# Chunked WKV attention into a gated MLP on one NeuronCore: the bonus term moved from v to the diagonal of the scores

## The chip, the cores and the metric

The program runs on one core of a Trainium2 chip. The metric is device time in microseconds of one execution, from launch to end. Three executions of the kernel before took 542.83, 542.98 and 543.75 us, so the median is 542.98 us.

## The reference

```python
# r, k, v: (4, 8, 768, 48); w, u: (8, 48); w_in: (384, 2048); w_out: (2048, 384)
for t in range(S):
    cur = einsum('bhd,bhe->bhde', u[None] * k_t, v_t)
    y[:, :, t] = einsum('bhd,bhde->bhe', r_t, state + cur)
    state = w[None, :, :, None] * state + einsum('bhd,bhe->bhde', k_t, v_t)
x = y.transpose(0, 2, 1, 3).reshape(3072, 384)
h = x @ w_in
out = (h * cos(h)) @ w_out
```

A recurrence over 768 time steps with a 48 by 48 state per head is followed by an MLP whose gate is h times cos h. The term with u, the bonus, reaches only the output of its own time step: for each time step and head it is the number a = sum over d of r u k, times the row v.

## The kernel before, in words

**Attention.** Time is cut into chunks of 128 steps; 4 batches of 6 chunks make 24 chunks, numbered i, with batch i mod 4 and place c = i div 4 in the batch. The function `chunk` (line 579) lays out one chunk for all 8 heads, as 4 pairs of heads. It loads k, r and v (lines 595 and 611), brings k and r with decays multiplied in to a layout with the head dimension on the partitions (kT, rT: on PE by transposes at line 653 for the first 12 chunks, on DVE at line 661 for the later 12), and lets PE make the scores, transposed, with 16 matmuls (`mm_a`, line 744). The scores of the even heads and the odd heads lie in two PSUM banks. A predicated copy on DVE (`mask`, line 750) writes the scores that lie strictly above the diagonal into a tile A in SBUF, which GpSimd had set to zero at the start (line 333). The output of the chunk, x transposed, is gathered in one PSUM bank from three parts: the bonus part, the part from the state z of earlier chunks (line 771, 24 matmuls, only where c is over 0), and A times v (`mm_x2`, line 784, 32 matmuls). From there it is split into a high and a low float32r half (lines 814 and 819), xh and xl. The state is brought on by 16 matmuls with k and v (line 830) and one or two DVE operations (lines 838 to 841).

**The bonus before.** Four elementwise steps make it: m = r times k (`o_m`, line 688), m times u (`o_mu`, line 717), a as the sum over each head (`o_a`, line 723), and m = v times a (`o_vm`, line 732; DVE for the first 12 chunks, GpSimd for the later ones). Then `mm_x` brings the 128 by 384 tile m into the PSUM bank with 3 PE transposes (line 763), ahead of the part from the state.

**MLP.** The 24 chunks form 8 blocks of 3 (384 tokens). A step is one block n and one 128-wide slice f of the hidden dimension: 9 matmuls give h (line 231), then ACT, DVE, ACT, ACT, DVE, ACT and DVE round the angle, reduce it, take its size, its sine, multiply the gate and split it into gh and gl (lines 242 to 251 and 942 to 948), and 9 matmuls add to the 3 accumulators (line 237). Each float32 product is made of three float32r products. Blocks 0 to 3 go through the slices in four groups (0 to 2, 2 to 5, 5 to 10, 10 to 16), since the weights are still being converted then; blocks 4 to 7 go through all 16 at once. The weights arrive as raw words and are converted by `conv` in 32 pieces (loads at 424 and 429, ACT 513, DVE 521 and 533, POOL 544, ACT 549, DVE 554).

**What sets the order.** Nothing is issued in the order in which it is written. Each operation is given to a planner (`Plan`, line 72) with an engine, a due time, a cost in us, a latency, the operations that it waits for and the buffers that it holds. The planner runs a list schedule: each engine takes, among the operations that could start earliest (within 0.01), the one with the lowest due time, and the resulting order is what each engine's queue gets, in order. Operations marked `port` are not planned beside each other, whether on DVE or POOL. Buffers are rings (2 for r, 3 for k and v, 4 for A, 8 for the general tile f that holds m, among others), and PSUM banks are handed out in the same way. Chunk i below 12 has due time -1.5 (12 - i) - 1; MLP step s has due time s. Ahead of the first h (line 1008) the gaps that the plan has on PE are filled with dummy matmuls (line 1002).

**The start.** DVE clears wr (line 339), SP loads w into it (line 348), PE transposes it (line 353), DVE raises it to powers (lines 361 to 368) and spreads them into the two decay tables decT_k (DVE, line 381) and decT_r (POOL, line 382). PE transposes decT_k and ACT copies it to dec_k (lines 390 and 394). u is spread to all partitions by a load (line 403). POOL makes the identity, clears the padding of the k, r and v tiles (`start_pool`), and then clears zt, makes the mask `upper` and clears A (`start_pool2`).

**The end.** Each finished accumulator is copied to SBUF (line 976 or 978) and stored: from SP where the group of slices began at slice 0 (line 984), which holds for the last block, else by an accumulating store from POOL (line 986).

Of the kernel before, what the change touches and what calls it, by code (L numbers as in the profile page):

```python
# [35 lines left out]
ON_DVE = (0, 0, 0, 12)  # L36
# [127 lines left out]
def kernel(  # L164
# [89 lines left out]
    with ExitStack() as actx:  # L254
# [63 lines left out]
        def start_pool2():  # L318
            for t in R_zt:
                nc.gpsimd.memset(t.ap, 0.0)  # L320

            nc.gpsimd.memset(upper, 1)
            nc.gpsimd.affine_select(
                out=upper,
                in_=upper,
                pattern=[[1, C]],
                compare_op=ALU.is_gt,
                fill=0,
                base=0,
                channel_multiplier=-1,  # L330
            )
            for t in R_A:
                nc.gpsimd.memset(t.ap, 0.0)

        def start_dve():
# [3 lines left out]
        o_wr = op(DVE, -100, 0.1, lambda: nc.vector.memset(wr, 1.0), lat=0.1)  # L339
# [9 lines left out]
            [o_wr],  # L349
# [3 lines left out]
        o_wT = op(PE, -95, 0.1, lambda: nc.tensor.transpose(b_w()[:, 0:NP], wr.rearrange("p j d -> p (j d)"), ident[0:NP, 0:NP]), [o_w, o_pool], [b_w], lat=0.3)  # L353
# [27 lines left out]
        o_dtk = op(DVE, -89, 0.6, lambda: spread_decay(nc.vector, decT_k, qk, rq), [o_pow])  # L381
        o_dtr = op(POOL, -89, 1.4, lambda: spread_decay(nc.gpsimd, decT_r, qr, pq), [o_pow])
# [9 lines left out]
        def tab_copy():  # L392
# [8 lines left out]
            -6.2,  # L401
# [177 lines left out]
        def chunk(i, due, xbuf):  # L579
# [60 lines left out]
            ahead = [o_pool, last_A[0]] if late else [o_pool]  # L640
# [6 lines left out]
            l_v = op(SP, due - 4.0, 1.35, load(vb, v), ahead, [vb], lat=2.6, line=ln)  # L647
# [24 lines left out]
            else:  # L672
                t_r = op(PE, due - 2.4, 0.43, tr(rTp, rb), [l_r], [rb, rTp, rT], lat=0.3)
# [24 lines left out]
            if first:  # L698
                t_k = op(PE, due - 2.5, 0.43, tr(kTp, kb), [l_k], [kb, kTp, kT], lat=0.3)
                e_k = op(  # L700
                    DVE,
                    due - 2.3,
                    0.62,
                    lambda: nc.vector.tensor_tensor(kT()[0:KP], cube(kTp)[0:KP], decT_k[0:KP], op=ALU.mult),
                    [t_k, o_dtk],
                    [kTp, kT],
                )
                o_kd = op(e2, due + 1.0, c2, decay_k, [t_k, o_m, o_dk], [kb], port=True)
            else:
                o_kd = op(e2, due - 2.7, c2, decay_k, [o_m, o_dk], [kb], port=True)  # L710
            if not first and not late:
                t_k = op(PE, due - 2.5, 0.43, tr(kTp, kb), [o_kd], [kb, kTp, kT], lat=0.3)
                e_k = op(ACT, due - 2.3, 0.5, lambda: nc.scalar.copy(kT()[0:KP], cube(kTp)[0:KP]), [t_k], [kTp, kT])
# [13 lines left out]
            e3, c3, n3 = on(3)  # L727
            o_vm = op(
                e3,
                due - 1.5,  # L730
                c3,
                lambda: n3.tensor_tensor(
                    heads(mb), vb()[:, :, 0:D], ab()[:, :, None].to_broadcast([P, H, D]), op=ALU.mult
                ),
                [o_a, l_v],
                [vb, ab, mb],
                port=True,
            )
# [7 lines left out]
            last_A[0] = o_A = op(PE, due - 1.7, 1.1, mm_a, [e_k, e_r], [kT, rT, *Ap, *A], lat=0.3)  # L746
# [7 lines left out]
            e_A = [op(DVE, due - 1.4 + 0.01 * j, 0.65, mask(j), [o_A, o_pool2], [Ap[j], A[j]]) for j in range(2)]  # L754
# [4 lines left out]
            def mm_x():  # L759
                x = xv()  # L760
                m2 = mb()
                for kk in range(NK):
                    nc.tensor.matmul(  # L763
                        x[:, kk, :], m2[:, kk * P : (kk + 1) * P], ident, is_transpose=True, start=(kk == 0), stop=False,
                        skip_group_check=True,
                    )
                if c:
                    for g in range(NK * 4):
                        p, s = divmod(g, 3)
                        gs = slice(G * (g % 4), G * (g % 4) + G)  # L770
                        nc.tensor.matmul(  # L771
                            x[gs, g // 4, :], zb()[:, p, G * s : G * s + G], rT()[0:KP, p, :], start=False, stop=False,
                            skip_group_check=True,
                        )

            def mm_x2():
                x = xv()
                for g in range(NK * 4):
# [4 lines left out]
                    for n, (j, at) in enumerate(parts):  # L783
# [4 lines left out]
                            start=False,  # L788
# [6 lines left out]
            if c:  # L795
# [6 lines left out]
            zbs = [zb] if c else []  # L802
            xo1 = op(
                PE,
                due - 0.7,
                0.42 + (0.8 if c else 0),
                mm_x,
                [o_vm, e_r, *e_A, *o_zt],
                [mb, rT, xp, *zbs],
                lat=0.3,  # L810
            )
            xo2 = op(PE, due - 0.65, 1.03, mm_x2, [xo1, l_v, *e_A], [vb, *A, xp], lat=0.3)
# [11 lines left out]
            if c < CPB - 1:  # L824
# [18 lines left out]
                zo = op(PE, due + 1.2, 0.5, mm_z, [o_kd, l_v, xo1], [kb, vb, zp], lat=0.3)  # L843
# [54 lines left out]
        for s, (n, f, f0, f1) in enumerate(steps):  # L898
# [62 lines left out]
            for t in range(nt):  # L961
# [6 lines left out]
                if f == f1 - 1:  # L968
# [13 lines left out]
                    def st(ob=ob, dst=dst, f0=f0):  # L982
                        if f0 == 0:
# [5 lines left out]
                        SP if f0 == 0 else POOL,  # L989
# [165 lines left out]
```

## Time and profile before

| | |
|---|---|
| median of three runs | 542.98 us (542.83 to 543.75) |
| the profiled execution, its own time | 543.04 us |
| its span, first to last instruction | 541.3 us |
| mean granted TensorE clock | 0.994 |
| PE matmul, busy | 525.1 us, 97% of the span |
| DVE, busy | 434.3 us, 80% |
| ACT, busy | 348.6 us, 64% |
| POOL, busy | 196.3 us, 36% |

The span is what the trace shows; 1.7 us of the execution's own time lie around it. Matmuls overlap in the pipeline, so the sum of their durations is more than PE's busy time, and the step from one start to the next is what a matmul takes of PE's time. In a row of the timeline stand the start in us, the duration in us, engine, line, operation, what is written and read, shapes and count, and in brackets the idle time of the engine ahead of it with what ended it. A merged row (x3) runs from the first start to the last end. In a row of groups the two numbers after the bar are the busy time of the group in us and the mean of one in ns.

### The profile page before, as it was taken

Reading aid. Unit: us, or ns where it says so; the run is one execution under the profiler, and the core shown is the slowest. Engines: PE = TensorE matmul, PEld = TensorE weight load, DVE = VectorE, ACT = ScalarE, POOL = GpSimd, SP = SyncE. Lnnn points to the kernel's source line nnn. Section 1 sums busy time; section 2 is a strip of 40 time slices with the busy share of each in tenths; the row PEclk is TensorE's granted clock in tenths of the full one; section 3 lists DMA queues with packets and bytes.
Section 4 is the critical chain, followed back from the end, with each engine's and each line's share of the span. In section 5 each row is a group of like instructions: output and inputs, shape, how many; then the busy total and the mean of one; then the engine's idle time right before and its main releaser. Section 6 shows DMA issues by size and latency. Waiting matters only on the chain.

```text
span 541.3 us, 11773 instructions
## 1 busy us (share of the span) xinstructions
PE 525.1 (97%) x4495; PEld 490.4 (91%) x4495; DVE 434.3 (80%) x846; ACT 348.6 (64%) x741; POOL 196.3 (36%) x201
## 2 busy tenths in 40 slices
PE   7998999999999999999999999999999999999995
PEld 5786889999899999999999999999989999999994
DVE  5988998888997876557788988998879898966543
ACT  2343556988788867756666666576665675666664
POOL 6768552254544353106244334503042254000000
PEclk9998999999999999999999999999999999999998
DMA  9788634656565684145466935637265555201001
GB/s 154 150 148 147 111 73 139 213 122 171 107 153 111 156 166 68 10 68 101 109 131 146 171 103 141 152 89 186 71 153 128 155 129 132 88 2 46 0 1 50
DMA packets 114979, 61.61 MB, mean 114 GB/s; under 512 B 78433, under 2 KB 110818, under 8 KB 114914
## 3 DMA queue, kind: packets, MB, share of 16 engines
q1 hardware_dynamic: 109730, 53.69, 40.9%
q0 software_dynamic: 5184, 7.08, 9.3%
q8 instruction: 37, 0.61, 0.5%
q14 instruction: 28, 0.23, 0.1%
HBM read 48.96 MB, written 11.80 MB: 112 GB/s over the span
## 4 chain that ended last, share of the span: by engine, by line
PE 84%; DVE 10%; issue 2%; ACT 2%; POOL 1%; DVEq 0%; ACTq 0%; POOLq 0%
PE bank L237 35%; PE bank L231 34%; PE bank L784 4%; PE bank L744 4%; PE bank L771 3%; PE bank L653 2%; DVE gl L948 2%; PE bank L830 1%; PE bank L763 1%; DVE f L245 1%; DVE A L750 1%; PE bank L1002 1%; DVE f L521 1%; DVE f L533 1%; DVE f L942 1%
## 5 line engine op out<-in xcount | busy, mean ns | idle before, releaser
L237 PE MATMUL bank<-w_out_hi,gh 128*128 128x384 f32 x384 | 132.0, 344 | 0.0
L237 PE MATMUL bank<-w_out_hi,gl 128*128 128x384 f32 x384 | 130.3, 339 | 1.6 <-DVE gl L948 1.5
L231 PE MATMUL bank<-xh,w_in_hi 128*128 128x384 f32 x384 | 131.7, 343 | 0.0
L237 PE MATMUL bank<-w_out_lo,gh 128*128 128x384 f32 x384 | 129.5, 337 | 0.0
L231 PE MATMUL bank<-xh,w_in_lo 128*128 128x384 f32 x384 | 129.3, 337 | 0.0
L231 PE MATMUL bank<-xl,w_in_hi 128*128 128x384 f32 x384 | 128.8, 335 | 0.0
L942 DVE TENSOR_TENSOR f<-bank,f 128x384 f32<-128x384 f32 (+1 forms) x132 | 71.2, 540 | 35.9 <-ACT f L251 35.3
L248 ACT ACTIVATE f<-f 128x384 f32<-128x384 f32 (+1 forms) x132 | 67.8, 515 | 48.9 <-DVE f L245 47.8
L948 DVE TENSOR_TENSOR gl<-f,gh 128x384 fp32r<-128x384 f32 (+1 forms) x132 | 79.6, 604 | 17.0 <-ACT gh L945 16.4
L242 ACT ACTIVATE qi<-bank 128x384 int32<-128x384 f32 (+1 forms) x132 | 62.6, 478 | 46.6 <-PE bank L231 46.3
L945 ACT CAST gh<-f 128x384 fp32r<-128x384 f32 (+1 forms) x132 | 65.9, 501 | 39.7 <-DVE f L942 35.7
L245 DVE SCALAR_TENSOR_TENSOR f<-bank,qi 128x384 f32<-128x384 f32 (+1 forms) x132 | 70.9, 539 | 24.9 <-ACT qi L242 23.8
L251 ACT ACTIVATE f<-f,quarter 128x384 f32<-128x384 f32 (+1 forms) x132 | 79.7, 606 | 2.7
L237 PEld LDWEIGHTS bank<-w_out_hi,gh 128*128 128x128 f32 x384 | 72.0, 187 | 4.7 <-issue 2.6
L231 PEld LDWEIGHTS bank<-xh,w_in_hi 128*128 128x128 f32 x384 | 72.1, 188 | 3.5 <-issue 2.0
L237 PEld LDWEIGHTS bank<-w_out_hi,gl 128*128 128x128 f32 x384 | 72.0, 188 | 3.2 <-DVE gl L948 3.0
L231 PEld LDWEIGHTS bank<-xl,w_in_hi 128*128 128x128 f32 x384 | 72.2, 188 | 0.0
L231 PEld LDWEIGHTS bank<-xh,w_in_lo 128*128 128x128 f32 x384 | 72.1, 188 | 0.0
L237 PEld LDWEIGHTS bank<-w_out_lo,gh 128*128 128x128 f32 x384 | 72.0, 187 | 0.0
L544 POOL TENSOR_TENSOR f<-f,raw 128x384 int32<-128x384 int32 x32 | 38.9, 1214 | 71.3 <-DVE f L533 34.9
L666 POOL TENSOR_TENSOR kT<-kT,decT_k 112x512 f32<-112x512 f32 x12 | 17.3, 1440 | 95.1 <-DVE kT L661 86.8
L986 POOL DMA_DIRECT2D out_dram<-f x36 | 32.9, 1195 | 30.6 <-ACT f L976 30.3
(92 smaller groups left out, 697.8 us busy)
## 6 DMA issues: line engine op xcount, KB each, us to landing
raw<-in_moe_w_in_dram SPq DMA_DIRECT2D x32, 384.0 KB, 3.6
raw<-in_moe_w_out_dram SPq DMA_DIRECT2D x32, 384.0 KB, 3.6
out_dram<-f POOLq DMA_DIRECT2D x36, 192.0 KB, 5.3
k<-in_k_dram SPq DMA_DIRECT2D x24, 192.0 KB, 4.0
v<-in_v_dram SPq DMA_DIRECT2D x24, 192.0 KB, 4.7
out_dram<-f SPq DMA_DIRECT2D x24, 192.0 KB, 2.1
raw<-in_k_dram SPq DMA_DIRECT2D x47, 96.0 KB, 2.3
raw<-in_r_dram SPq DMA_DIRECT2D x47, 96.0 KB, 2.4
```

The lines of the kernel that those rows point to most:

```text
L231: nc.tensor.matmul(ph, a, b_, start=(i == 0), stop=(i == len(mm) - 1))
L237: nc.tensor.matmul(acc, a[:, ts], b_[:, f, :], start=(first and i == 0), stop=(last and i == 2))
L242: nc.scalar.activation(qi, ph, AF.Copy, scale=INV_2PI)
L245: nc.vector.scalar_tensor_tensor(q, ph, INV_2PI, qi, op0=ALU.mult, op1=ALU.subtract)
L248: nc.scalar.activation(q, q, AF.Abs)
L251: nc.scalar.activation(q, q, AF.Sin, scale=-TWO_PI, bias=quarter)
L544: lambda: nc.gpsimd.tensor_tensor(ai(), ai(), cn(), op=ALU.add),
L744: nc.tensor.matmul(cube(Ap[j])[:, p, :], kT()[ps, p, :], rT()[ps, p, :], start=True, stop=True)
L942: nc.vector.tensor_tensor(g()[:, cs], ph()[:, cs], q()[:, cs], op=ALU.mult)
L945: nc.scalar.copy(gh()[:, cs], g()[:, cs])
L948: nc.vector.tensor_tensor(gl()[:, cs], g()[:, cs], f32(gh())[:, cs], op=ALU.subtract)
L986: nc.gpsimd.dma_start(dst, ob(), accum_op=ALU.add)
```

## The change

The bonus becomes part of A. Since `mm_x2` multiplies A by v, a on the diagonal of A gives a times v. ACT now fills each A tile with the identity times a, head by head (8 activations of 128 by 128 a chunk, `diagonal`), so that A is zero off the diagonal, and the mask then writes the scores above the diagonal over it. With that go the product v times a, the 3 transposes, and GpSimd's clearing of A at the start.

```diff
-ON_DVE = (0, 0, 0, 12)
+ON_DVE = (0, 0, 0)
...
-            for t in R_A:
-                nc.gpsimd.memset(t.ap, 0.0)
...
-            e3, c3, n3 = on(3)
-            o_vm = op(
-                e3,
-                due - 1.5,
-                c3,
-                lambda: n3.tensor_tensor(
-                    heads(mb), vb()[:, :, 0:D], ab()[:, :, None].to_broadcast([P, H, D]), op=ALU.mult
-                ),
...
+            def diagonal(j):
+                def go():
+                    for p in range(NP):
+                        h = 2 * p + j
+                        nc.scalar.activation(A[j]()[:, p, :], ident, AF.Copy, scale=ab()[:, h : h + 1])
...
+            o_d = [op(ACT, due - 1.55 + 0.01 * j, 0.9, diagonal(j), [o_a, o_pool], [ab, A[j]], line="diagonal") for j in range(2)]
...
-            last_A[0] = o_A = op(PE, due - 1.7, 1.1, mm_a, [e_k, e_r], [kT, rT, *Ap, *A], lat=0.3)
+            last_A[0] = o_A = op(PE, due - 1.7, 1.1, mm_a, [e_k, e_r], [kT, rT, *Ap], lat=0.3)
...
-            e_A = [op(DVE, due - 1.4 + 0.01 * j, 0.65, mask(j), [o_A, o_pool2], [Ap[j], A[j]]) for j in range(2)]
+            e_A = [op(DVE, due - 1.4 + 0.01 * j, 0.65, mask(j), [o_A, o_d[j], o_pool2], [Ap[j], A[j]]) for j in range(2)]
...
-                for kk in range(NK):
...
-                        x[:, kk, :], m2[:, kk * P : (kk + 1) * P], ident, is_transpose=True, start=(kk == 0), stop=False,
...
+                        x[gs, g // 4, :], zb()[:, p, G * s : G * s + G], rT()[0:KP, p, :], start=(g < 4), stop=False,
...
-                            start=False,
+                            start=(not c and g < 4 and n == 0),
...
-            xo2 = op(PE, due - 0.65, 1.03, mm_x2, [xo1, l_v, *e_A], [vb, *A, xp], lat=0.3)
+            xo1 = None
+            if c:
+                xo1 = op(PE, due - 0.7, 0.8, mm_x, [e_r, *e_A, *o_zt], [rT, xp, zb], lat=0.3)
+            xo2 = op(PE, due - 0.65, 1.03, mm_x2, [xo1, l_v, o_pool, *e_A], [vb, *A, xp], lat=0.3)
...
-                zo = op(PE, due + 1.2, 0.5, mm_z, [o_kd, l_v, xo1], [kb, vb, zp], lat=0.3)
+                zo = op(PE, due + 1.2, 0.5, mm_z, [o_kd, l_v, o_A], [kb, vb, zp], lat=0.3)
```

The other edits concern the start and the end. The load of w no longer waits for DVE's clearing of wr, which now touches only the padding. decT_r is made on DVE, after decT_k, and both are planned as using the shared port. The load of u has its due time moved from -6.2 to -23.9, that of each v from 4.0 to 5.0 ahead of its chunk's. The loads of k, r and v wait no longer for POOL's start; the PE operations that read the padding wait for it instead. The last store of all is issued by ACT.

```diff
-            [o_wr],
+            [],
...
-        o_dtk = op(DVE, -89, 0.6, lambda: spread_decay(nc.vector, decT_k, qk, rq), [o_pow])
-        o_dtr = op(POOL, -89, 1.4, lambda: spread_decay(nc.gpsimd, decT_r, qr, pq), [o_pow])
+        o_dtk = op(DVE, -89, 0.65, lambda: spread_decay(nc.vector, decT_k, qk, rq), [o_pow], port=True)
+        o_dtr = op(DVE, -88, 0.65, lambda: spread_decay(nc.vector, decT_r, qr, pq), [o_pow], port=True)
...
-            -6.2,
+            -23.9,
...
-            ahead = [o_pool, last_A[0]] if late else [o_pool]
+            ahead = [last_A[0]] if late else []
...
-            l_v = op(SP, due - 4.0, 1.35, load(vb, v), ahead, [vb], lat=2.6, line=ln)
+            l_v = op(SP, due - 5.0, 1.35, load(vb, v), ahead, [vb], lat=2.6, line=ln)
...
+                        if last:
+                            nc.scalar.dma_start(dst, ob())
```

More of the change, by code (lines that the diff above doesn't have):

```diff
@@ L337, in start_dve @@
             nc.vector.memset(pq[:, :, 0:1], 1.0)
-        o_wr = op(DVE, -100, 0.1, lambda: nc.vector.memset(wr, 1.0), lat=0.1)
+        o_wr = op(DVE, -100, 0.1, lambda: nc.vector.memset(wr[:, :, D:DP], 1.0), lat=0.1)
         o_pool = op(POOL, -99, 1.7, start_pool)
@@ L352 @@
         b_w = Buf(B_EARLY)
-        o_wT = op(PE, -95, 0.1, lambda: nc.tensor.transpose(b_w()[:, 0:NP], wr.rearrange("p j d -> p (j d)"), ident[0:NP, 0:NP]), [o_w, o_pool], [b_w], lat=0.3)
+        o_wT = op(PE, -95, 0.1, lambda: nc.tensor.transpose(b_w()[:, 0:NP], wr.rearrange("p j d -> p (j d)"), ident[0:NP, 0:NP]), [o_w, o_wr, o_pool], [b_w], lat=0.3)
         def mul(dst, a, b_):
@@ L672, in chunk @@
             else:
-                t_r = op(PE, due - 2.4, 0.43, tr(rTp, rb), [l_r], [rb, rTp, rT], lat=0.3)
+                t_r = op(PE, due - 2.4, 0.43, tr(rTp, rb), [l_r, o_pool], [rb, rTp, rT], lat=0.3)
                 e_r = op(
@@ L698, in chunk @@
             if first:
-                t_k = op(PE, due - 2.5, 0.43, tr(kTp, kb), [l_k], [kb, kTp, kT], lat=0.3)
+                t_k = op(PE, due - 2.5, 0.43, tr(kTp, kb), [l_k, o_pool], [kb, kTp, kT], lat=0.3)
                 e_k = op(
@@ L711, in chunk @@
             if not first and not late:
-                t_k = op(PE, due - 2.5, 0.43, tr(kTp, kb), [o_kd], [kb, kTp, kT], lat=0.3)
+                t_k = op(PE, due - 2.5, 0.43, tr(kTp, kb), [o_kd, o_pool], [kb, kTp, kT], lat=0.3)
                 e_k = op(ACT, due - 2.3, 0.5, lambda: nc.scalar.copy(kT()[0:KP], cube(kTp)[0:KP]), [t_k], [kTp, kT])
@@ L760, in mm_x @@
                 x = xv()
-                m2 = mb()
-                for kk in range(NK):
+                for g in range(NK * 4):
+                    p, s = divmod(g, 3)
+                    gs = slice(G * (g % 4), G * (g % 4) + G)
                     nc.tensor.matmul(
-                        x[:, kk, :], m2[:, kk * P : (kk + 1) * P], ident, is_transpose=True, start=(kk == 0), stop=False,
+                        x[gs, g // 4, :], zb()[:, p, G * s : G * s + G], rT()[0:KP, p, :], start=(g < 4), stop=False,
                         skip_group_check=True,
                     )
[L767 to L774, printed above, removed]
             def mm_x2():
@@ L980, with st @@
                     oc = op(ACT if t % 2 == 0 else DVE, s + 2.3, 0.45, cp, [oo], [acc[t], ob])
-                    def st(ob=ob, dst=dst, f0=f0):
-                        if f0 == 0:
+                    last = jc == NJ - 1
+                    def st(ob=ob, dst=dst, f0=f0, last=last):
+                        if last:
+                            nc.scalar.dma_start(dst, ob())
+                        elif f0 == 0:
                             nc.sync.dma_start(dst, ob())
@@ L988 @@
                     stored[jc] = op(
-                        SP if f0 == 0 else POOL,
+                        ACT if last else SP if f0 == 0 else POOL,
                         s + 2.5,
```

15 lines of the change are left out of this document (1 added, 14 removed).

## The prediction

> **What bounds the kernel now.** I read the page first, then busy time by stage, then the chain of waits in two halves, then the timeline of the start. Engine sums (busy us, share, count), then stages (from:to, length, busy us of PE, its weight loads, DVE, ACT and POOL, granted clock, DMA share, GB/s):
>
> ```profile
> PE 525.1 (97%) x4495; PEld 490.4 (91%) x4495; DVE 434.3 (80%) x846; ACT 348.6 (64%) x741; POOL 196.3 (36%) x201
> ...
> 12.83:49.70 36.87, 32.64 (x550) 26.83 (x550) 32.19 (x59) 14.67 (x31) 25.91 (x25) 1.00 0.80 146
> 49.70:90.00 40.30, 40.27 (x629) 33.51 (x630) 36.14 (x71) 21.93 (x48) 20.14 (x18) 0.96 0.49 106
> 90.00:220.00 130.00, 128.57 (x734) 127.62 (x733) 107.58 (x207) 105.97 (x231) 55.41 (x54) 1.00 0.61 139
> 220.00:480.00 260.00, 259.80 (x2219) 242.06 (x2218) 218.88 (x415) 165.53 (x341) 86.29 (x80) 1.00 0.50 118
> ```
>
> The share of PE hides two regimes. From 49.7 us on PE hardly pauses: 40.27 of 40.30, 128.57 of 130, 259.80 of 260. Before that it waits: 32.64 of 36.87 counts dummy matmuls too. The chain says the same. Its half before 49.7, by line, then its half after, then some pieces of it (start, length, what):
>
> ```profile
> by line: DVE A L750 9.1%; PE bank L1002 8.5%; PE bank L653 6.2%; issue 6.0%; DVE rT L678 5.2%; POOL f L717 5.1%; DVE f L521 5.0%; DVE a L723 4.9%; DVE f L732 4.7%; PE bank L744 4.5%; PE bank L784 4.2%; PE bank L231 3.6%; DVE zc L841 3.4%; D
> ...
> by line: PE bank L237 38.1%; PE bank L231 36.9%; PE bank L784 3.9%; PE bank L744 3.6%; PE bank L771 3.0%; DVE gl L948 1.7%; issue 1.6%; PE bank L830 1.4%; PE bank L763 1.3%; DVE f L245 1.2%; PE bank L653 1.1%; ACT f L248 0.5%; DVE f L942 0.
> ...
> 45.21 1.52 POOL f L717
> ...
> 46.75 0.55 DVE a L723
> ...
> 49.20 0.48 DVE f L732
> ...
> 49.73 0.59 PE bank L763 x3
> ...
> 58.55 0.33 PE bank L763 x3
> ```
>
> In the first half DVE steps lead (masks, decay products, sums), with PE between them; DVE is busy 32.19 of 36.87 us, 87%, POOL 70%, ACT 40%. In the second half the MLP's matmuls hold 75% and attention's matmuls most of the rest, so a PE instruction removed there is time removed, and one removed in the first half is not.
>
> **The change part by part.**
>
> *The 3 transposes.* A piece of three is 0.33 us on the chain. The first and the last ahead of 49.7, then the group, and that of v times a:
>
> ```profile
> 17.16 0.55 PE L763 MATMUL bank<-ident,f 128*128 128x128 f32 x3 [0.95 <-DVE f L732]
> ...
> 42.78 0.49 PE L763 MATMUL bank<-ident,f 128*128 128x128 f32 x3
> ...
> L763 PE MATMUL bank<-ident,f 128*128 128x128 f32 x72 | 12.0, 276 | 2.9 <-DVE f L732 2.9
> L732 DVE TENSOR_TENSOR f<-v,a 128x384 f32<-128x384 f32 x12 | 9.2, 766 | 0.1
> ```
>
> There are 72, so 24 pieces; 6 begin before 49.7, from 17.16 to 42.78, and 18 after. 18 x 0.33 = 5.9 us; the chain's 1.3% of the 491.6 us behind 49.7 is 6.4, with the two slower pieces. I take 5.9, since the slow ones were slow for other reasons.
>
> *v times a.* In the late chunks it is on POOL, 33% busy there, off the path: nothing. In the early ones it costs DVE about 0.48 us each on the chain (the mean of 766 ns counts contention). Seven of twelve start before 49.7: 7 x 0.48 = 3.4 us off an engine that is 87% busy and heads the chain. The rest of the front (POOL's two products and decay a chunk, loads) doesn't shrink with it, so I take 2.5, with bounds 0 and 3.4.
>
> *The start.* The timeline, from SP's first issues to the first score matmul:
>
> ```profile
> 0.83 0.46 SPq L424 DMA_DIRECT2D raw<-in_moe_w_in_dram  x1
> 1.35 0.84 SPq L348 DMA_DIRECT2D wr<-in_w_dram  x1
> 2.24 0.40 SPq L403 DMA_DIRECT2D u_b<-in_u_dram  x1
> 2.67 0.43 SPq L595 DMA_DIRECT2D k<-in_k_dram  x1
> 3.74 1.92 POOL L333 MEMSET A<- 128x512 f32 x4
> 5.43 0.26 PE L353 MATMUL bank<-ident,wr 4*128 4x4 f32 x1
> 8.64 1.11 POOL L374 TENSOR_TENSOR decT_r<-qr,pq 128x512 f32<-128x512 f32 x1 [2.99 <-DMA r<-in_r_dram]
> 8.74 1.56 DVE L374 TENSOR_TENSOR decT_k<-qk,rq 128x512 f32<-128x512 f32 x1
> 10.36 0.66 PE L390 MATMUL bank<-ident,decT_k 128*128 128x128 f32 x4 [1.74 <-DVE decT_k L374]
> 12.83 1.16 PE L744 MATMUL bank<-rT,kT 48*128 48x128 f32 x16 [0.84 <-DVE rT L678]
> 22.69 0.55 DVE L554 TENSOR_TENSOR w_in_lo<-f,w_in_hi 128x384 fp32r<-128x384 f32 x1
> ...
> 31.95 0.45 PE L231 MATMUL bank<-xh,w_in_hi 128*128 128x384 f32 x1
> ...
> L678 DVE TENSOR_TENSOR rT<-bank,decT_r 112x512 f32<-112x512 f32 x12 | 8.2, 683 | 1.7 <-PE bank L653 1.7
> ...
> out_dram<-f SPq DMA_DIRECT2D x24, 192.0 KB, 2.1
> ```
>
> Before, w was held by DVE's clearing, so SP issued 384 KB of raw weights first, and w, issued at 1.35, was used at 5.43, 4.1 us later. Now w goes first, at 0.83, with nothing ahead of it; the quickest landing in the trace is 2.1 us (the plain stores), so its transpose starts near 3.3 instead of 5.43: 2.1 us. decT_r now follows decT_k on DVE. The 1.56 us of decT_k ran beside POOL's 1.11; alone a product of that width is 0.68 (decay of rT), so two in a row are about 1.5 and cost nothing against 1.56, at worst 1.5 more. k, r and v move ahead of raw, and POOL, without 1.92 us of clearing, begins its products sooner. I take 2.0 for the first scores' advance (0.5 to 3.5). The price is that the first raw load stands behind u and two chunks, perhaps ten us later. Its cover: the converted piece is ready at 22.69 + 0.55 and first used at 31.95, 8.7 us of slack, and while h waits PE has attention to do. I cost it at nothing; without cover, 1 to 2 us.
>
> *The diagonal.* 8 ACT instructions a chunk, reading SBUF, with a scale from a column. The nearest rows:
>
> ```profile
> L251 ACT ACTIVATE f<-f,quarter 128x128 f32<-128x128 f32 x6 | 2.2, 392 | 0.1
> L945 ACT CAST gh<-f 128x128 fp32r<-128x128 f32 x6 | 1.6, 291 | 0.1
> L242 ACT ACTIVATE qi<-bank 128x384 int32<-128x384 f32 x126 | 61.4, 487 | 46.1 <-PE bank L231 45.8
> ...
> 530.07 0.60 ACT L242 ACTIVATE qi<-bank 128x128 int32<-128x128 f32 x3
> 531.45 0.68 ACT L251 ACTIVATE f<-f,quarter 128x128 f32<-128x128 f32 x2
> ```
>
> The sine takes its bias from a column: 0.39 us, and two in 0.68, so one every 0.29. Without a column operand it is 0.29, and three in 0.60 gives one every 0.16. No row has a scale from a column; I take 0.29, the row with a column operand, so a chunk costs 8 x 0.29 = 2.3 us (1.3 at the least). Against ACT's room: 14.67 + 7 x 2.3 = 31 of 36.87; 21.93 + 5 x 2.3 = 33 of 40.30; nothing in 90 to 220; 165.53 + 12 x 2.3 = 193 of 260. ACT becomes fuller, but nowhere the fullest.
>
> The Trainium skill ("ScalarE: Activation LUTs", What ACT_TABLE_LOAD costs) gives each column operand, scale or bias, 93 ns and back-to-back activations an overlap of 93 ns, which by my estimate is 293 ns of spacing at 128 columns. The trace agrees for the bias, 0.39 against 0.29 and a spacing of 0.29; for a scale no run here shows it yet. Were the column free, the sum below would lose its stall term.
>
> *The wait that it adds.* The plan gives a group of four fills 0.9 us; at 0.29 apart it is 3 x 0.29 + 0.39 = 1.26, so each group ends 0.36 later than planned. DVE's mask now waits for it, and DVE runs in order: behind the mask stand the next chunk's decay product and sum and the MLP's gate steps; behind A, the 24 and 32 matmuls of the output. In the late chunks A is made well ahead of its block, and I charge nothing. In the twelve early ones I charge half a group's overrun: 12 x 0.18 = 2.2 us; bounds 0, if DVE is late itself at the mask, and 12 x 0.72 = 8.6, if it waits out both.
>
> *The rest.* The score matmuls no longer wait for an A tile and the state matmuls no longer for the output: earlier only. The last store:
>
> ```profile
> 535.04 0.48 ACT f L976
> ...
> L984 SPq DMA_DIRECT2D out_dram<-f x3: 333/335/388, 534.5 to 535.5; - x3
> ```
>
> ACT makes the copy that ends at 535.52 and now issues its store. SP was free by then, so this saves a hand-over at most; no row has an ACT store. Bounds -0.1 and +0.5, taken as 0, the issue being 0.34 on SP.
>
> *Sum*, on the profiled execution's 543.0 (the median is 542.98, no difference): 543.0 - 5.9 - 2.5 - 2.0 + 2.2 = 534.8, so **535**.
>
> **The rivals.**
>
> *The front isn't DVE's.* POOL's step and the sum behind it are on the chain too (45.21, 46.75), and POOL keeps all three products of a chunk. Then the front's 4.5 us aren't gained: 543.0 - 5.9 + 2.2 = 539.3. Against it: 70% against 87% busy.
>
> *More than the sum.* After the wait that ends with v times a at 49.20 + 0.48 = 49.68, PE runs slow:
>
> ```profile
> 48.00:50.00 2.00, 0.27 (x2) 0.28 (x3) 1.97 (x4) 0.24 (x1) 1.92 (x2) 1.00 1.44 167
> 50.00:52.00 2.00, 2.00 (x29) 1.34 (x28) 2.00 (x4) 0.15 (x1) 1.50 (x2) 0.53 0.93 121
> 52.00:54.00 2.00, 2.00 (x36) 1.52 (x34) 1.53 (x2) 1.14 (x3) 1.77 (x2) 0.62 0.96 220
> ```
>
> If the gap (2.0 - 0.27 = 1.7 us) goes, and the 0.53 and 0.62 of clock with it (2 x 0.47 + 2 x 0.38 = 1.7 us), and the masks never wait, it is 534.8 - 3.4 - 2.2 = 529.2.
>
> *Slower: the mask behind ACT.* Place: DVE's queue, at the first mask of a chunk, in late chunks as well, where DVE has 219 of 260 us. If the two groups' overrun, 0.72 us, falls on PE in every chunk, that is 24 x 0.72 = 17.3 and the time 543.0 - 10.4 + 17.3 = 550. The gains of 10.4 are gone at 10.4 / 24 = 0.43 us a chunk, and it is slower by more than the bound at 0.48; my sum has 0.09. For it speaks that two engines must now meet in the plan's order with a cost set 0.36 too low, against it that A is needed only by the last part of the output and that other costs of the plan are short too (the rounding step, 0.487 us in the rows, is planned at 0.39) and PE is still full.
>
> The Trainium skill ("ScalarE: Activation LUTs", Rules for kernel authors) tells one to put multiplications on VectorE, not ScalarE, and so speaks against this edit. The trace would have one DVE product of 512 columns at 0.68 for four fills at 1.26, but on the engine at 87% in place of the one at 40%; by the rule the edit falls to this rival.
>
> **How the numbers follow.** A measurement here can tell about 0.2%, 1.1 us. Forecast (531 to 537.5) 0.53; front not gained (537.5 to 541.9) 0.20; more than the sum (527 to 531) 0.12; gains eaten (541.9 to 544.1) 0.05; slower 0.10. Faster is 0.53 + 0.20 + 0.12 = 0.85. The range, 529 to 541.5, leaves out the slower rival, the even case and a corner of the fourth: under 0.2. It spans the unknown costs: 534.8 - 2.2 - 3.4 = 529.2 below, 534.8 + 8.6 - 2.2 = 541.2 above.
>
> **What would show it.** Right: no transposes of f by ident; 192 ACT fills near 0.39 us, ACT busy about 24 x 2.3 = 55 us more; w's transpose near 3.3 and first scores near 10.8; PE unbroken from near 45; the stretch behind 220 shorter by 12 x 0.33 = 4 us. Wrong: waits of DVE's masks on ACT in the list of waits with PE idle behind them, a first h that waits for its converted weights, or a front that still ends at 49.7.

## The result and the profile after

| | before | changed |
|---|---|---|
| median, us | 543.75 (542.83 to 544.09, 5 runs) | 530.1 (528.75 to 530.91, 5 runs) |
| ratio, with its 95% interval | 1 | 0.9749 (0.9731 to 0.9767) |
| the profiled execution, us | 543.04 | 530.91 |
| its span, us | 541.3 | 529.2 |

The changed kernel is 2.5% faster, 13.6 us in the medians and 12.1 us in the two spans, against the 8 us of the forecast. The time lies inside the range of 529 to 541.5, but outside the forecast's own 531 to 537.5, in the band of the rival called "more than the sum" (527 to 531, worked out at 529.2).

The page's engine sums of the changed kernel:

```profile
PE 515.1 (97%) x4428; PEld 481.2 (91%) x4428; DVE 424.9 (80%) x835; ACT 397.8 (75%) x933; POOL 178.4 (34%) x184
```

Busy time by stage (from:to, length, busy us of PE, its weight loads, DVE, ACT and POOL, granted clock, DMA share, GB/s); the second half ends at 470, where the last stage of the MLP has not begun:

```profile
12.83:49.70 36.87, 36.01 (x696) 29.12 (x694) 29.13 (x57) 31.14 (x93) 24.53 (x25) 1.00 0.83 153
49.70:90.00 40.30, 39.68 (x482) 35.63 (x481) 34.30 (x71) 35.03 (x89) 16.25 (x17) 1.00 0.44 128
...
210.00:470.00 260.00, 257.53 (x2196) 240.13 (x2195) 222.50 (x421) 191.60 (x434) 76.74 (x69) 1.00 0.50 118
```

Between 12.83 and 49.7 PE now holds 36.01 us of 36.87 (32.64 before, dummy matmuls counted in both), DVE 29.13 (32.19), and ACT 31.14 where 31 were worked out (14.67 before). The granted clock between 49.7 and 90 is 1.00 and not 0.96. Behind 210, though, PE is idle for 2.5 us of 260, where before it was idle for 0.2.

The groups of the fills and of the masks, and the waits that belong to them (busy us and mean ns, then idle time ahead and what ended it; in the list of waits: us in total, times, the longest):

```profile
L730 ACT ACTIVATE A<-ident,a 128x128 f32<-128x128 f32 x192 | 59.3, 389 | 6.3 <-DVE a L721 5.8
...
L746 DVE COPY_PREDICATED A<-upper,bank 128x512 f32<-128x512 int32 x48 | 34.9, 741 | 8.1 <-ACT A L730 6.4 <-PE bank L812 0.7 <-PE bank L740 0.3
```

```profile
DVE A L746 <- ACT A L730: 6.4, 9, 1.4
...
ACT A L730 <- DVE a L721: 5.8, 7, 1.7
...
PE bank L231 <- DVE f L924: 2.8, 3, 1.7
...
PEld bank L773 <- DVE A L746: 0.9, 2, 0.7
```

The new wait is there: DVE stood at its masks for 6.4 us, in nine places. But it hardly reaches PE: the weight loads of the output matmuls waited 0.9 us for a mask. What PE waits for instead is a gate step of the MLP (line 924), 2.8 us in three places, one of 1.67.

The timeline of the changed kernel, at the start, at the output matmuls of chunks 11 and 12, at the longest pause of PE and at the end:

```profile
0.83 0.84 SPq L346 DMA_DIRECT2D wr<-in_w_dram  x1
...
1.73 0.42 SPq L593 DMA_DIRECT2D k<-in_k_dram  x1
...
3.63 0.26 PE L351 MATMUL bank<-ident,wr 4*128 4x4 f32 x1
...
7.45 0.68 DVE L372 TENSOR_TENSOR decT_k<-qk,rq 128x512 f32<-128x512 f32 x1
8.05 0.68 DVE L372 TENSOR_TENSOR decT_r<-qr,pq 128x512 f32<-128x512 f32 x1
...
9.99 1.16 PE L740 MATMUL bank<-rT,kT 48*128 48x128 f32 x16 [0.49 <-DVE rT L676]
...
10.59 2.45 ACT L730 ACTIVATE A<-ident,a 128x128 f32<-128x128 f32 x8 [1.23 <-DVE a L721]
...
32.26 1.72 SPq L422 DMA_DIRECT2D raw<-in_moe_w_in_dram  x1
...
64.41 0.45 PE L231 MATMUL bank<-xh,w_in_hi 128*128 128x384 f32 x1
...
66.86 1.08 PE L773 MATMUL bank<-A,v 128*32 128x128 f32 x32
...
229.61 1.10 PE L773 MATMUL bank<-A,v 128*32 128x128 f32 x32
...
391.32 2.16 DVE L456 TENSOR_TENSOR f<-f,f 128x384 f32<-128x384 f32 x1
...
393.98 0.55 DVE L924 TENSOR_TENSOR f<-bank,f 128x384 f32<-128x384 f32 x1
...
394.58 0.44 PE L231 MATMUL bank<-xh,w_in_hi 128*128 128x384 f32 x1 [1.67 <-DVE f L924]
...
522.89 0.48 ACT L958 COPY f<-bank 128x384 f32<-128x384 f32 x1 [0.56 <-PE bank L237]
...
523.40 0.38 ACTq L969 DMA_DIRECT2D out_dram<-f  x1
```

The output matmuls of the same two chunks in before:

```profile
85.83 1.10 PE L784 MATMUL bank<-A,v 128*32 128x128 f32 x32
...
240.06 1.10 PE L784 MATMUL bank<-A,v 128*32 128x128 f32 x32
```

The rows at 66.86 and 85.83 are the output matmuls of chunk 11, the last of the early ones; those at 229.61 and 240.06 are chunk 12's, the first of the late ones. They cut a kernel's time into three parts. **Front**: up to chunk 12's output matmuls. **Back**: from there to the last copy of an accumulator (522.89 here, 535.04 before). **End**: from that copy to the end of the span. Front, back and end are 229.6, 293.3 and 6.3 us in the changed kernel and 240.1, 295.0 and 6.3 us before. So 10.4 us of the 12.1 come from the front, 1.7 from the back and none from the end. By the forecast's own terms the front, which holds chunk 12's three transposes too, should have given 7 x 0.33 + 2.5 + 2.0 - 2.2 = 4.6 us and the back 11 x 0.33 = 3.6. The mark is sound: in every kernel below, 903 of the 2304 matmuls of the MLP lie ahead of it.

One thing looks quite unlike the forecast: the first raw weights are loaded at 32.26, not ten us later than before's 0.83, and the first h runs at 64.41 and not at 31.95. PE did attention first, and the MLP later.

### The profile page after: what moved, and what is told of

It reads as the page before. It is cut to its first block, busy times and chain, and to the rows that moved or that the text cites. A ratio compares the mean times of both kernels' runs of the same rounds, so it can differ in the third digit from the quotient of the medians.

```text
span 529.2 us, 11825 instructions
## 1 busy us (share of the span) xinstructions
PE 515.1 (97%) x4428; PEld 481.2 (91%) x4428; DVE 424.9 (80%) x835; ACT 397.8 (75%) x933; POOL 178.4 (34%) x184
## 4 chain that ended last, share of the span: by engine, by line
PE 81%; DVE 8%; ACT 5%; issue 2%; DMA 2%; POOL 1%; SPq 0%; DVEq 0%; ACTq 0%; POOLq 0%
PE bank L231 33%; PE bank L237 32%; PE bank L740 5%; PE bank L773 5%; PE bank L760 3%; PE bank L651 2%; PE bank L812 2%; DVE gl L930 2%; DMA raw<-in_moe_w_out_dram 1%; DVE f L924 1%; ACT A L730 1%; PE bank L989 1%; ACT gh L927 1%; DVE f L245 1%; ACT f L251 1%
## 5 line engine op out<-in xcount | busy, mean ns | idle before, releaser
L930 DVE TENSOR_TENSOR gl<-f,gh 128x384 fp32r<-128x384 f32 (+1 forms) x132 | 84.2, 641 | 14.2 <-ACT gh L927 12.9
L730 ACT ACTIVATE A<-ident,a 128x128 f32<-128x128 f32 x192 | 59.3, 389 | 6.3 <-DVE a L721 5.8
L664 POOL TENSOR_TENSOR kT<-kT,decT_k 112x512 f32<-112x512 f32 x12 | 15.6, 1302 | 143.5 <-DVE kT L659 111.8
```

The lines of the kernel that those rows point to most:

```text
L730: nc.scalar.activation(A[j]()[:, p, :], ident, AF.Copy, scale=ab()[:, h : h + 1])
L930: nc.vector.tensor_tensor(gl()[:, cs], g()[:, cs], f32(gh())[:, cs], op=ALU.subtract)
```

## The experiments

Three theories were to be told apart. *Work*: the gain is the work taken from PE and DVE, as the forecast summed it. *Order*: the gain comes from waits that the planner no longer has to plan around, above all the state matmuls (they waited for the output and now wait for the scores only), which set free k's and v's buffers earlier, so that attention's loads pass the weights' and the weights' conversions leave the front. *Start*: the early loads and tables carry it. For the edits three letters: **S** the edits of the start, **Z** the state matmuls' earlier wait, **D** the diagonal (with the end's store on ACT). The changed kernel is S, Z and D together.

| kernel | edits | front, us | back, us | end, us | median, us | ratio to before (95%) | gain, us |
|---|---|---|---|---|---|---|---|
| before | none | 240.1 | 295.0 | 6.3 | 543.75 | 1 | 0 |
| e1_start_only | S | 231.9 | 295.4 | 7.3 | 536.32 | 0.9847 (0.9808 to 0.9886) | 8.3 |
| e9_before_z_early | Z | 234.6 | 294.8 | 7.9 | 539.39 | 0.9909 (0.9874 to 0.9944) | 4.9 |
| e13_diag_alone | D | 231.5 | 292.8 | 7.8 | 533.99 | 0.9811 (0.9793 to 0.9829) | 10.3 |
| e10_start_z | S Z | 234.7 | 294.7 | 7.5 | 538.3 | 0.9894 (0.987 to 0.9917) | 5.8 |
| e8_z_late | S D | 235.6 | 292.8 | 7.6 | 537.72 | 0.9887 (0.9859 to 0.9915) | 6.1 |
| e2_diag_only | Z D | 233.4 | 294.0 | 5.9 | 534.9 | 0.9824 (0.9799 to 0.985) | 9.6 |
| changed | S Z D | 229.6 | 293.3 | 6.3 | 530.1 | 0.9749 (0.9731 to 0.9767) | 13.6 |
| e11_tables | part of S | 232.4 | 295.0 | 7.6 | 536.41 | 0.986 (0.9836 to 0.9884) | 7.6 |
| e7_before_hold | weights held | 237.1 | 295.5 | 7.2 | 541.46 | 0.996 (0.9943 to 0.9977) | 2.2 |
| e12_before_dummies | dummies | 238.1 | 295.4 | 7.6 | 542.53 | 0.9973 (0.9961 to 0.9984) | 1.5 |
| e3_early_only | S Z, D early only | 229.1 | 294.8 | 5.8 | 531.87 | 0.9786 (0.9762 to 0.981) | 11.6 |
| e4_true_cost | S Z D, costlier in the plan | 230.6 | 291.6 | 7.7 | 532.42 | 0.9802 (0.9779 to 0.9825) | 10.8 |
| e5_diag_dve | S Z, D on DVE | 237.5 | 296.4 | 5.9 | 540.03 | 0.9918 (0.9899 to 0.9936) | 4.5 |

The gain is what the ratio leaves of 543.75. The parts are of each kernel's profiled execution; the end, which only stores, scatters between 5.8 and 7.9 us whichever engine issues the last store, so single spans can't be compared closer than that.

**The start alone** (e1_start_only): before, with

```diff
-        o_wr = op(DVE, -100, 0.1, lambda: nc.vector.memset(wr, 1.0), lat=0.1)
+        o_wr = op(DVE, -100, 0.1, lambda: nc.vector.memset(wr[:, :, D:DP], 1.0), lat=0.1)
...
-        o_dtr = op(POOL, -89, 1.4, lambda: spread_decay(nc.gpsimd, decT_r, qr, pq), [o_pow])
+        o_dtr = op(DVE, -88, 0.65, lambda: spread_decay(nc.vector, decT_r, qr, pq), [o_pow], port=True)
...
-            ahead = [o_pool, last_A[0]] if late else [o_pool]
+            ahead = [last_A[0]] if late else []
```

and the other edits of the start, the bonus as it was.

> The kernel before with the edits of the start alone: w first, decT_r on DVE, u early, loads of k, r and v that don't wait for POOL, v one us earlier in the plan; the bonus as before. Theory A (work taken off the engines: product of v and a off DVE, transposes off PE, sets the gain): only the start's 2 to 3 us, so 541. Theory B (the gain of the front comes from the order: state matmuls that no longer wait for the chunk's output free k and v sooner, so attention's loads pass the raw weights and conversions leave the front): 541 too, with raw loads still between the loads of k, r and v. Theory C (the start edits carry it): 537 or less.

Measured: 8.3 us (6.2 to 10.4), all in the front. This is far over the forecast's 2.0 for the start, and over the bound of 3.5, with the first scores at 9.88.

**The diagonal without the start** (e2_diag_only): the changed kernel with those edits put back (D and Z).

> The changed kernel with the start put back: raw weights first, w behind DVE's clearing, decT_r on POOL, loads behind POOL's start. Diagonal, early state matmuls and the last store on ACT stay. Theories A and B: 532 to 533, the start's 2 to 3 us given back. Theory C: 537 or more.

Measured: a gain of 9.6 us. So the start and the rest are each worth over half of the whole 13.6, and their sum (8.3 + 9.6) is more than it.

**The diagonal in the early chunks only** (e3_early_only): the changed kernel, with v times a and the 3 transposes back in chunks 12 to 23.

```diff
-            o_d = [op(ACT, due - 1.55 + 0.01 * j, 0.9, diagonal(j), [o_a, o_pool], [ab, A[j]], line="diagonal") for j in range(2)]
...
+            if not late:
+                o_d = [op(ACT, due - 1.55 + 0.01 * j, 0.9, diagonal(j), [o_a, o_pool], [ab, A[j]], line="diagonal") for j in range(2)]
+            elif i < XS + 2:
+                o_d = [op(POOL, due - 1.55 + 0.01 * j, 0.53, clear(j), [o_a], [A[j]]) for j in range(2)]
```

> The changed kernel with the diagonal in the first 12 chunks only; chunks 12 to 23 have the product of v and a on POOL and the three transposes again, and POOL clears the A tiles once between. If 12 x 0.33 us of transposes are time removed behind 220 us, 534; if the fills on ACT cost there what the transposes save, as the lag of 1.2 us between the two traces over that stretch suggests, 530 to 531.5.

Measured: a gain of 11.6, 2.0 us less than the changed kernel, where the 12 late pieces are 4.0. Its busy time by stage says where the rest went:

```profile
210.00:470.00 260.00, 259.80 (x2220) 242.38 (x2219) 220.22 (x417) 165.61 (x341) 87.80 (x82) 1.00 0.50 118
```

With its transposes PE is busy for 259.80 of 260; without them, in the changed kernel, for 257.53. So 2.3 us of the 4 saved turn into pauses. The front is the same to 0.5 us, so it is the early diagonals that count there.

**The state matmuls wait again** (e8_z_late): the changed kernel with one line altered.

```diff
-                zo = op(PE, due + 1.2, 0.5, mm_z, [o_kd, l_v, o_A], [kb, vb, zp], lat=0.3)
+                zo = op(PE, due + 1.2, 0.5, mm_z, [o_kd, l_v, xo1, *e_A], [kb, vb, zp], lat=0.3)
```

> The changed kernel, in which the state matmuls wait again for the masks and for the state's part of the output, as the kernel before had it by way of xo1. Nothing else differs. Theory A: 530 to 532, within 2 us of the changed kernel. Theory B: 536 or more, first h near 32 us again and conversions between the first chunks.

Measured: a gain of 6.1 us, so this one wait is worth 7.5 us in the changed kernel. Weights come early again (first raw loads at 12.69 and 18.47, first h at 26.24), and PE pauses late in the front. The pause, and the stretch behind it:

```profile
47.87 0.44 PE L237 MATMUL bank<-w_out_hi,gl 128*128 128x384 f32 x1 [2.22 <-DVE gl L930]
```

```profile
50.00:52.00 2.00, 2.00 (x28) 1.58 (x28) 1.16 (x2) 1.52 (x4) 1.45 (x2) 0.50 0.43 85
```

The clock is 0.50 here, as it was near 0.5 in before behind its pause of 1.98 us:

```profile
49.73 0.59 PE L763 MATMUL bank<-ident,f 128*128 128x128 f32 x3 [1.98 <-DVE f L732]
```

**The same wait in before** (e9_before_z_early): before with only that edit the other way round, `[o_kd, l_v, xo1]` to `[o_kd, l_v, o_A]`.

> The kernel before with one edit: the state matmuls wait for the score matmuls instead of for the first part of the output. No work is removed. Theory A: 543 to 544, no gain. Theory B: 537 to 539, with the attention loads ahead of the raw weights and the first h after 55 us.

Measured: a gain of 4.9 us (3.0 to 6.9) from what the forecast had called "earlier only" and counted as nothing. The longest pause in this part is 1.49 us and the clock stays at 1.00. The weights move as the theory of the order says, though less:

```profile
0.83 0.45 SPq L424 DMA_DIRECT2D raw<-in_moe_w_in_dram  x1
...
26.08 0.70 SPq L429 DMA_DIRECT2D raw<-in_moe_w_out_dram  x1
...
34.38 0.45 PE L231 MATMUL bank<-xh,w_in_hi 128*128 128x384 f32 x1
```

The second raw load goes from 16.05 to 26.08.

**The weights held back by hand** (e7_before_hold): before, with all raw loads waiting for the scores of chunk 4.

```diff
-HOLD = ()
+HOLD = (4,) * 32
```

> The kernel before, with every load of raw weights held back until chunk 4 is done and nothing else changed. If conversions in the front are what slows it (theory B), 538 to 540; if the conversions only fill idle slots, 543 to 546, or slower, since the first steps then wait for weights.

Measured: only 2.2 us (1.3 to 3.1), with the first raw load at 44.10 and the first h at 57.23. So the front isn't shortened by late weights as such: the pause and the slow clock are gone (1.98 + 1.7), and with no raw load ahead of w the first scores come at 10.35 and not at 12.83, yet the gain is less than these together. The theory of the order is right that the wait counts, but its chain through the weights isn't borne out.

**Start and state matmuls without the diagonal** (e10_start_z): before with S and Z.

> The kernel before with the start edits and the early state matmuls, but with the bonus as before: product of v and a, three transposes a chunk. The difference from the changed kernel (530) is the worth of the diagonal. Theory A (removed work): 537 or more, since 24 transpose groups and 12 products on DVE come back. Theory B (order): 532 to 534, the diagonal being worth little. The single effects (7.7 for the start, 4.6 for the state matmuls) would add up to 531.7.

Measured: 5.8 us, not more than S alone. The reason stands in its timeline and its stages: a late pause, here at a matmul of h that waits for its converted weight (the first h ran at 66.31), and a slow stretch behind it.

```profile
71.72 0.69 PE L231 MATMUL bank<-xh,w_in_hi 128*128 128x384 f32 x1 [2.54 <-ACT w_in_hi L549]
```

```profile
72.00:74.00 2.00, 2.00 (x7) 1.91 (x8) 1.64 (x4) 0.73 (x2) 0.17 (x1) 0.50 0.66 197
74.00:76.00 2.00, 2.00 (x11) 2.00 (x10) 0.47 (x1) 0.89 (x2) 0.85 (x1) 0.72 0.08 8
```

**The tables only** (e11_tables): before with w loaded first, the clearing of wr cut to its padding and decT_r on DVE, without the edits of u, k, r and v.

> The kernel before with w loaded first, wr's clearing cut to the padding and decT_r on DVE; the loads of k, r, v and u as before. If the start edits' 7.7 us come from the tables, 537; if they come from the loads that no longer wait for POOL and go ahead of the raw weights, 541 to 542, the advance of the first scores alone.

Measured: 7.6 us, the same as S within the intervals. The early loads add nothing that shows; the first scores are at 10.33 here against 9.88.

**Dummies in the pause** (e12_before_dummies): before with 14 dummy matmuls ahead of chunk 6's output, where PE paused for 1.98 us.

```diff
+                if i == 6:
+                    warm_up(14)
```

> The kernel before with 14 dummy matmuls on PE ahead of the transposes of chunk 6, where PE pauses for 2.0 us at 47.7 and then runs for 3.4 us at half the clock. Nothing else is moved; the pause itself stays. If the pause causes the half clock, the clock stays at 1.00 and the time falls by half of 3.4, 1.7 us. If the half clock comes of something else or is hidden by what follows, no change.

Measured: 1.5 us (0.9 to 2.1). The dummies fill most of the pause, and the stretch behind it is at full clock:

```profile
47.08 1.70 PE L1004 MATMUL bank<-warm 128*128 128x256 bf16 x14
...
49.05 0.55 PE L765 MATMUL bank<-ident,f 128*128 128x128 f32 x3 [0.27 <-DVE f L732]
```

```profile
50.00:52.00 2.00, 2.00 (x53) 1.43 (x43) 1.97 (x4) 1.28 (x3) 1.16 (x2) 1.00 1.00 145
52.00:54.00 2.00, 2.00 (x36) 1.70 (x36) 2.00 (x3) 0.48 (x1) 1.92 (x3) 1.00 0.69 208
```

Before had 0.53 and 0.62 in these two rows. The transposes behind the pause begin 0.68 us earlier than in before (49.05 against 49.73), and the front ends 2.0 us earlier; so 1.3 us are gained behind the pause, where the clock is what differs: the slow clock's price, forecast at 1.7. This isn't one execution alone: the mean granted clock is 0.996 or 0.997 in all seven of this kernel, 0.993 or 0.994 in the eleven of before beside them.

**The diagonal alone** (e13_diag_alone): the changed kernel with the start put back and the state matmuls waiting again.

> The changed kernel with both the start edits and the early state matmuls put back: diagonal on ACT, no product of v and a, no transposes (and the last store on ACT). The kernel before is at 543.7 with a half clock stretch in it. If the diagonal is worth its own sum (5.9 for transposes, 2.5 for DVE, less 2.2 for waits), 537 to 538; if removed work turns to waits as long as the order of the loads stays, 541 to 544.

Measured: 10.3 us (9.3 to 11.3), more than the forecast for the whole change. In the profiled execution 8.6 us are the front's and 2.2 the back's, with the end 1.5 longer.

**A truer cost in the plan** (e4_true_cost): the changed kernel with a group of four fills planned at 1.2 us and not 0.9.

> The changed kernel with each group of four fills planned at 1.2 us, near the 1.26 that it takes, in place of 0.9. If the overrun costs what the prediction charged (2.2 us) or more, 528 or less; if DVE's waits at the masks are hidden, 530 with the scatter that another order brings, about 1.5 us either way.

Measured: 10.8 us, 2.9 less than the changed kernel. The front is 1.0 us longer, the back 1.7 shorter, the end 1.4 longer. The plan's wrong cost therefore isn't what costs time, and a plan as close as this one differs by 1 to 2 us in either part, with nothing saved or added in work. Part of the 2.9 is the clock: two of its four executions took 531.64 and 531.75 us at a mean clock of 0.997, the others 533.11 at 0.993 and 534.64 at 0.991; the changed kernel's five had 0.997 to 0.999.

**The diagonal on DVE** (e5_diag_dve): the changed kernel with each group of four fills made by one DVE product.

```diff
-                    for p in range(NP):
-                        h = 2 * p + j
-                        nc.scalar.activation(A[j]()[:, p, :], ident, AF.Copy, scale=ab()[:, h : h + 1])
+                    aj = ab().rearrange("q (p j) -> q p j", j=2)[:, :, j : j + 1]
+                    nc.vector.tensor_tensor(
+                        A[j](), ident[:, None, :].to_broadcast([P, NP, C]), aj.to_broadcast([P, NP, C]), op=ALU.mult
+                    )
```

> The changed kernel with the diagonal filled by DVE: one product of the identity and a broadcast of a for four heads, 128 by 512, two a chunk, in place of eight fills on ACT. ACT loses 2.3 us a chunk, DVE gains about 2 x 0.68. If ACT with its column operand is the dearer place, faster than 530; if DVE's fullness decides, as the prediction had it, 12 x 1.3 = 16 us of DVE's time come into the front and the time is 534 to 540.

Measured: 4.5 us, so it is 9.2 us slower than with the fills on ACT. Its stages and its group of fills:

```profile
12.83:49.70 36.87, 34.98 (x651) 27.71 (x652) 36.77 (x65) 12.42 (x28) 29.66 (x26) 1.00 0.87 149
...
210.00:470.00 260.00, 254.90 (x2125) 237.61 (x2123) 232.33 (x430) 164.12 (x341) 77.42 (x70) 1.00 0.51 118
```

```profile
L729 DVE TENSOR_TENSOR A<-ident,a 128x512 f32<-128x512 f32 x48 | 36.2, 780 | 0.0
```

A group costs DVE 0.78 us where ACT needs 1.27 (3 x 0.294 + 0.389, below), yet DVE is busy for 36.77 of 36.87 us in the front, and PE idle for 5.1 of 260 in the back. A pause of 2.75 us late in the front, followed by a half clock for 6.8 us, is part of the loss:

```profile
74.98 0.69 PE L231 MATMUL bank<-xh,w_in_hi 128*128 128x384 f32 x1 [2.75 <-ACT w_in_hi L547]
```

## Why the prediction was right or wrong, step by step

**The sign was right, and DVE's share in the front in part.** Every kernel with the diagonal on ACT was faster than before. The first rival (the front isn't DVE's, 539.3) isn't borne out: with the diagonal alone (e13) the front is 8.6 us shorter. But the 2.5 us for v times a were not a general relief of DVE. In before PE waited twice in the front for this product, 2.9 us in all (the group row of the transposes), and the longer wait is the pause of 1.98. So the forecast's 2.5 and the rival's gap of 1.7 price the same wait twice. e5 agrees only in part: with the fills on DVE, DVE has no room left in the front, but most of the 7.9 us more are pauses and slow clock (table below).

**The price of a fill was right.** The forecast took 0.39 us and one every 0.29. Measured: 389 ns, and the eight of the first chunk in 2.45 us, (2.45 - 0.389) / 7 = 0.294 us apart. ACT is busy for 397.8 - 348.6 = 49.2 us more (55 forecast). The Trainium skill ("ScalarE: Activation LUTs", What ACT_TABLE_LOAD costs), which gives each column operand, scale or bias, the same price, agrees: the sine with its bias took 392 ns before.

**The transposes: right in sum, wrong in place.** The forecast took 18 pieces at 0.33 us: 7 in the front, 2.3 us, and 11 in the back, 3.6 us. Eight kernels with these transposes (before, e1, e3, e7, e9 to e12) have backs of 294.7 to 295.5, the mean 295.0; five with ACT fills in their place 291.6 to 294.0, the mean 292.9. So they are worth 2.1 us there. "From 49.7 us on PE hardly pauses, so a PE instruction removed there is time removed" held only as long as nothing else came up to PE's pace; DVE was at 219 of 260 us, and a gate step on it can come late once PE is quicker. In the timeline above the longest pause ends with a gate step that had stood behind a product of 2.16 us and a sum on DVE. "One removed in the first half is not" doesn't hold either: by the table below PE's steps in the front shrink by 3.6 us in the mean of the kernels with D, more than the 2.3 of 7 pieces and near 13 x 0.33 = 4.3 for all 13. That 3.6 + 2.1 = 5.7 comes out near the 5.9 of the forecast is luck.

**The wait at the masks: mis-sized, 2.2 forecast.** DVE waits for ACT as described, 6.4 us in nine places, but PE behind it only 0.9, and a truer plan gains nothing (e4). Take 0 for it, the lower bound. The slower rival, "the mask behind ACT", asked for 0.43 us a chunk on PE; it got 0.9 / 24 = 0.04. In its favour stood the rule of the Trainium skill to put multiplications on VectorE ("ScalarE: Activation LUTs", Rules for kernel authors), which gives its reason for bf16 and goes by the time of one element. Here, in float32, the measurement decides against that rule: DVE's product is shorter, and the kernel 9.2 us slower with it.

**The start: its dates right, its worth not.** w's transpose starts at 3.63 (3.3 forecast), the first scores at 9.99 (10.8, from 12.83), and the two tables follow each other on DVE at 0.68 each as estimated. But a gain of 2.8 us in the first scores isn't the start's worth: the fronts of e1 and e11 are 8.2 and 7.6 us shorter. Part is before's pause of 1.98 us and the slow clock behind it (1.7), which neither has there (e1 has a pause of 2.05 us later, at full clock); the rest, 4.5 and 3.9 us, is the scores' advance (2.9 and 2.5) and some 1.5 us in smaller pauses and shorter steps of PE, which no run explains.

**The pause and the slow clock: counted as a rival, and it came.** The forecast left this out of its sum (chance 0.12 for the rival). The changed kernel has neither: its longest pause is 1.67 us, and the clock is 1.00 from 4.1 to 526.3. e12 shows the slow clock's part alone, 1.3 us of the forecast 1.7.

**"Earlier only", taken as 0: this step failed.** The state matmuls' new wait is worth 4.9 us on before (e9) and 7.5 us in the changed kernel (e8). Some of each is the pause and the slow clock again (3.7 us in before; 2.22 + 1.7 in e8); what is left in the front is 5.5 - 3.7 = 1.8 and 5.9 - 3.9 = 2.0 us. That remainder was in no term of the sum. No work is removed by this edit, and by the table below its worth is a matter of pauses, dummies and slow clock; the other steps of PE don't shrink with it.

**The raw load: the cover held, the distance didn't.** It was to stand ten us later and stands 31 later; a cost of its own doesn't show: PE does attention meanwhile, and no matmul's wait for a converted weight stands in the changed kernel's list of waits. No run tests it by itself.

**The last store: 0, as taken.** The end is 6.3 us in both.

**The front in parts.** The time up to chunk 12's output matmuls can be counted out on PE: up to the first scores, then PE's pauses, the dummies, half of each stretch at half clock, and the steps of everything else (a step is the time from one start to the next, less a pause). Pauses are the length less PE's busy time, first in before, then in the changed kernel:

```profile
12.83:240.06 227.23, 221.55 (x2053) 207.00 (x2053) 187.11 (x356) 155.77 (x336) 104.08 (x99) 0.99 0.60 126
...
9.99:229.61 219.62, 216.82 (x2026) 202.65 (x2026) 177.39 (x346) 181.78 (x440) 99.30 (x98) 1.00 0.63 134
```

| kernel | edits | first scores at, us | pauses | dummies | slow clock | other steps |
|---|---|---|---|---|---|---|
| before | none | 12.8 | 5.7 | 3.0 | 1.7 | 216.9 |
| e1_start_only | S | 9.9 | 2.4 | 4.2 | 0 | 215.4 |
| e9_before_z_early | Z | 12.3 | 3.3 | 2.2 | 0 | 216.8 |
| e13_diag_alone | D | 12.8 | 3.7 | 3.0 | 0 | 212.0 |
| e10_start_z | S Z | 10.0 | 4.2 | 3.2 | 1.7 | 215.5 |
| e8_z_late | S D | 9.9 | 8.2 | 3.5 | 1.7 | 212.2 |
| e2_diag_only | Z D | 12.6 | 4.5 | 2.5 | 0 | 213.9 |
| changed | S Z D | 10.0 | 2.8 | 4.6 | 0 | 212.2 |
| e5_diag_dve | S Z, D on DVE | 9.9 | 7.1 | 6.6 | 3.4 | 210.5 |

From before to the changed kernel the front's 10.4 us are 2.8 in the first scores, 2.9 in pauses, 1.7 in the slow clock and 4.7 in the other steps, less 1.7 for more dummies; with 1.7 of the back that makes the 12.1 of the two spans. In the forecast's terms: 2.0 for the start was 2.8; 2.3 for the front's transposes was 4.7 (3.6 in the mean of the four kernels with D against the four without); against 2.5 for the product less 2.2 for the masks stand 2.9 of pauses less 1.7 of dummies; the slow clock's 1.7 was left out of the sum; and the back's 3.6 was 1.7. The rival "more than the sum" had the slow clock right, but its 529.2 beside 530.1 rests on the gap that it counts twice, on masks without a wait, and on a back that it has too short; that it came so near is in part luck.

**What stays open.** The edits don't add: S, Z and D by themselves gain 8.3, 4.9 and 10.3 us, 23.5 together, and all three in one kernel 13.6. The table says why. Two parts go with their edit in whatever company: S brings the first scores forward by 2.3 to 3.0 us, and D takes 3 to 5 us off the other steps. Z brings the first scores forward by 0.5 us at most and takes nothing off the other steps. The rest is pauses, dummies and slow clock, and these three sum to 10.3 us in before, to between 5.4 and 9.2 in the kernels with S, Z, D, S Z or Z D, to 13.4 with S D and to 7.4 in the changed kernel. Before's pause and slow clock, 3.7 us, can be gained only once, and each of S, Z and D by itself gains them. All five pauses of about 2 us or more (before, e1, e5, e8, e10) lie behind the kernel's first h, up to which the planner fills its gaps with dummies. Why a plan has more or fewer such waits isn't explained by any run here; e4 shows that a change of a planned cost alone moves the front and the back by 1 to 2 us. The parts are each of one execution.

## What to carry to other kernels

When a planner or a list schedule orders the work, price not only the instructions that go but also the waits that go: try the single dependence by itself, as it may be worth as much as the work. Where single gains don't add up, count pauses, fillers and slow clock in each variant: a pause that every edit removes is gained once. Count a gain on the busiest engine in full only as far as the next one has room there (here 2.1 of 3.6 us were left). Move a per-partition scaling to the engine with room even where its instructions are dearer, and look at the clock's column behind every pause of the matrix engine of about two us.

## What the runs showed of the hardware

Pauses of PE shorter than the slow stretch that followed them were enough to halve the granted clock: 1.98 us in before, 2.22 in e8 and 2.54 in e10, each with a stretch of 3.41 us at half clock that began 0.4, 1.5 and 0.0 us behind the pause's end, and 2.75 in e5 with 6.83. A pause of 2.05 us in e1 had no such stretch:

```profile
66.06 0.44 PE L231 MATMUL bank<-xh,w_in_hi 128*128 128x384 f32 x1 [2.05 <-DVE xl L819]
```

The traces show what sets them apart. In all 14 of them the clock changes only at points that are a multiple of 3.41 us apart (in before it is full from 5.73 to 50.11, 13 times 3.41 us, half to 53.52, and full to 538.21). On that grid before's pause lies in one interval, e8's all but 0.3 us, e1's is cut by the line at 64.84. PE's busy time of such intervals in before, in e8 and three times in e1 (interval, length, busy, granted clock in it, DMA share, GB/s):

```profile
46.70:50.11 3.41, 1.43 (x19) 1.00 1.44 167
...
45.98:49.39 3.41, 1.52 (x21) 1.00 0.78 180
...
61.43:64.84 3.41, 2.58 (x64) 1.00 0.30 50
64.84:68.25 3.41, 2.19 (x13) 1.00 0.35 118
525.64:529.05 3.41, 1.54 (x8) 1.00 0.34 117
```

Behind the first two, idle for 1.98 and 1.89 us, the clock is 0.50; behind the last three, idle for 0.83, 1.22 and 1.87, it is 1.00. From the first full clock on every interval of the 14 traces fits: idle for 1.89 us or more is followed by half clock, for 1.87 or less by full. The one exception is in e5, where an interval already at half clock, 0.67 us idle, is followed by half again, so what brings the clock back isn't settled here. The Trainium skill ("TensorE: Matmul & The Clock Gate", What's actually happening) has the clock fall after an idle window of about 3.4 us, with windows that run freely, 3413 ns long. The grid agrees with that; that the window be idle does not, since 1.89 of 3.41 us were enough. So whether a pause of about two us costs half clock depends on where the grid cuts it, and the grid's first full clock stands between 4.1 and 6.9 us in these traces.
